# Two row tiles for the first MoE's turned rows, row stores ahead of the loads, and an earlier load of the branch value

## The chip, the cores and the metric

The kernel runs on one core of one Trainium2 chip. The metric is the device time of one execution in microseconds (us); three runs of the kernel before gave 932.9, 933.44 and 936.52, median 933.44. The execution that the profile shows took 933.06, and its span (first to last instruction) is 930.8; the 2.3 between them lies outside the instructions.

## The reference, cut to what matters

Attention over 4 batches of 12 heads (448 tokens, head size 64) with capped scores, then a dense gated MLP ("first MoE", 768 to 1536 to 768), then a routed MoE with 8 experts. All in float32.

```
scores = cap * tanh(q @ k.T / 8 / cap); attn = softmax(scores); x = attn @ v     # cap = 30
x = (silu(x @ w_gate) * (x @ w_val)) @ w_out                                    # 1792 x 768
do = x @ w_skip > 0; e = argmax(x[do] @ w_route); g = softmax prob of e
out = x;  out[do] += g * (relu(x[do] @ w1[e]) @ w2[e])
```

## The kernel before, in words

**Staging.** The 48 heads are worked in 24 pairs. The dense MLP works on one batch (448 tokens) at a time, in 36 units per batch: 12 of gate, 12 of value, 12 of output columns (6 blocks of 128 columns, each in two halves, in the order y00 y10 y01 y11 y20 y21 ...). A unit is 18 matmuls of 448 columns, since each product is made of three (high by high, low by high, high by low; `mm3`, L680 to L683). The attention of the next batch is woven between the units of this one, so that TensorE always has one or the other.

**The weights.** In the first batch they come as raw 64-bit words, 768 KB a unit (`load_w`, L629). ScalarE takes the absolute value (L639), VectorE clamps (L643) and puts the bits together (L648, L651, L654), and the 32-bit weight is kept in DRAM (`keep_w`, L678). Later batches load it from there, two units at a time (L620). Of each weight, ScalarE makes the rounded part wh (L668) and VectorE the rest wl (L356), both two units ahead of their product.

**The rows.** When an output block of 128 columns is done, ScalarE copies it out of PSUM (x2, L728). `turn_rows` (L747) lets TensorE make its routing logits (L751) and VectorE transpose it in 32 by 32 blocks into a tile "row" (L756). One unit later `store_rows` (L758) sends the row to the output with four transfers from SyncE's queue, 56 KB each, in runs of 32 floats (L762). Before the change the pool behind "row" has one buffer, so the transpose of the next block waits until the four stores of the block before have landed.

**What sets the order.** There is no scheduler: each engine works its instructions off in the order in which the program issues them. The order is written out by hand in lists of words. `OPENING` starts the first pairs; `unit(w)` (L1125) goes through `FIRST_UNITS` in the first batch and `UNITS` afterwards, and calls the function that stands behind each word in `place` (L1108). "store" is `store_rows` for the block that ended three units back, "rows" is `turn_rows` for the one that ended two back, "piece", "keep" and "loads" issue the loads of weights, the keeping of them and the loads of q, k and v. All of these transfers go out on SyncE's one queue, in program order, and each of them waits for the transfer eight before it. The sums of the softmax of a pair come from TensorE (L548), VectorE turns them (dn, L573) and TensorE spreads them again (L579); all further work of TensorE stands behind that matmul.

**The start.** The first pair's q and k are transposed by TensorE (L1287) and copied (L1290). Then each engine loads the value `big` (is the cap large?) into a register (L1291) and branches on it (L1292); with a cap of 30 the branch goes to `whole(False)`.

Of the kernel before, what the change touches and what calls it, by code (L numbers as in the profile page):

```python
# [7 lines left out]
F32 = mybir.dt.float32  # L8
# [41 lines left out]
""".split()  # L50
FIRST_UNITS = """
    out weigh sum scores1 roundw bits gate hidden after after after bits loww dn products both bits tanh1 exp1
    tanh2 exp2 turn abs bits split last bits scores2 bits piece keep loads logits count rows chain turnl store
""".split()
UNITS = """
    out turnl weigh sum scores1 scores2 products fold count logits rows hidden split loads tanh1 exp1 add1 turn
# [13 lines left out]
def tile_attn_moe_moe(  # L70
# [15 lines left out]
    nc = tc.nc  # L86
    B, H, S, D = q.shape
# [22 lines left out]
    big_i = const.tile([128, 1], I32, name="big_i")  # L110
# [15 lines left out]
    count = const.tile([T, E], F32, name="count")  # L126
# [9 lines left out]
    rows = const.tile([T, 128], mybir.dt.bfloat16, name="rows")  # L136
# [226 lines left out]
    def load_block(g, i):  # L363


        b, h = divmod(2 * g, H)
        a, j, e = i // 4, i // 2 % 2, i % 2
        qkn = block_of(g)
        p0 = 64 * j + 32 * e
        nc.sync.dma_start(  # L370
            out=qkn[p0:p0 + 32, a],
            in_=(q, k)[a][b, h + j, :, 32 * e:32 * e + 32].rearrange("(c i) d -> i c d", i=32),
        )
        return qkn

    def first_pair():
        return head_room[0:T, 0:2 * NC * 128].rearrange("p (a c h d) -> p a c h d", a=2, c=NC, h=2)

    def first_turned():
        return pair_room[1][:, 2 * S:4 * S].rearrange("p (a s) -> p a s", a=2)  # L380

    def whole(exact):
        with ExitStack() as ph:
# [13 lines left out]
            one_p = pool("one", 1)  # L397
# [287 lines left out]
            cur, terms = {}, {}  # L685
# [61 lines left out]
            def turn_rows(b, j):  # L747
                x2 = cur.pop(("x2", j))
                cur["lp", j] = lp = ps_m.tile([128, T], F32, name="mo")
                for c in range(NC):  # L750
                    nc.tensor.matmul(  # L751
                        lp[32 * c:32 * c + 32], lhsT=w9[:, j], rhs=x2[:, T * c:T * c + T], start=True, stop=True
                    )

                cur["row", j] = row = so["row"] if b == B - 1 and j % 2 else one_p.tile([128, S], F32, name="row")
                nc.vector.transpose(out=row, in_=x2)  # L756

            def store_rows(b, j):  # L758
# [58 lines left out]
            chain = [None, None]  # L817
# [13 lines left out]
            so = {"raw": [], "pair": [], "xg": [], "auto": False}  # L831
# [269 lines left out]
            def chain_on(w):  # L1101
# [10 lines left out]
                "scores1": of_head(1, scores, 3), "scores2": of_head(5, scores, 4),  # L1112
                "products": lambda w: w < W_END and products(w), "count": lambda w: step("p", 1),
                "logits": of_rows(add_logits, 3), "turnl": of_rows(turn_logits, 4), "rows": of_rows(turn_rows, 2),
                "store": of_rows(store_rows, 3), "split": split_due, "last": split_last, "loads": loads,
                "chain": chain_on, "tanh1": of_head(0, tanh, 2), "exp1": of_head(0, exp, 2),
# [24 lines left out]
            for word in OPENING:  # L1141
                name = word.rstrip("0123456789")
# [92 lines left out]
    with tc.manual_schedule():  # L1235
        nc.sync.dma_start(out=cap_sb, in_=cap.to_broadcast([128, 1]))
        for i, (queue, src) in enumerate(((nc.sync, q), (nc.scalar, k))):
            for j in range(2):
                queue.dma_start(out=first_pair()[:, i, :, j], in_=src[0, j].rearrange("(c p) d -> p c d", c=NC))
        for i in range(8):  # L1240
            load_block(1, i)
        nc.gpsimd.memset(ident, 1.0)
        nc.gpsimd.affine_select(
            out=ident, in_=ident, pattern=[[1, 128]], compare_op=ALU.is_equal, fill=0.0, base=0,
            channel_multiplier=-1,
        )
        nc.vector.memset(ones, 1.0)
        nc.scalar.activation(out=old, in_=ones[0:T, 0:1], func=ACTF.Tanh)
        nc.vector.tensor_reduce(
            alike[:, 0], ident.rearrange("p (a b) -> p b a", b=32), axis=AX.X, op=ALU.add  # L1250
        )
        nc.vector.tensor_copy(alike[:, 1], alike[:, 0])
        nc.vector.memset(w9, 0.0)
        nc.vector.tensor_scalar(big_i, cap_sb, cap_sb, CAP_FAST * CAP_FAST, op0=ALU.mult, op1=ALU.is_gt)
        nc.vector.tensor_scalar(inv_sb, cap_sb, float(D) ** 0.5, None, op0=ALU.mult)
        nc.vector.reciprocal(inv_sb, inv_sb)

        with tc.tile_pool(name="setup", bufs=5) as setup:

            def count_off(dst, **kw):  # L1260
                ti = setup.tile(list(dst.shape), I32, name="ti")
                nc.gpsimd.iota(ti[:], **kw)
                nc.vector.tensor_copy(dst, ti)

            count_off(rank8, pattern=[[-1, E]], base=E, channel_multiplier=0)
            count_off(rows, pattern=[[1, 128]], base=1, channel_multiplier=0)
            count_off(steps, pattern=[[128, JM]], base=0, channel_multiplier=0)
            count_off(slots, pattern=[[1, MAXSLOT]], base=0, channel_multiplier=0)
            nc.vector.tensor_scalar(number, rank8, -1.0, float(E), op0=ALU.mult, op1=ALU.add)
            nc.vector.tensor_tensor(  # L1270
                before, rank8.unsqueeze(1).to_broadcast([T, E, E]), rank8.unsqueeze(2).to_broadcast([T, E, E]),
                op=ALU.is_gt,
            )

            count_off(tok, pattern=[[T, NT]], base=-65536, channel_multiplier=1)
            nc.gpsimd.memset(oh, 0.0)
            nc.gpsimd.memset(above, 0.0)
            nc.gpsimd.affine_select(
                out=lt, in_=ones[0:T], pattern=[[1, T]], compare_op=ALU.is_ge, fill=0.0, base=0,
                channel_multiplier=-1,  # L1280
            )

        with tc.tile_pool(name="first", bufs=2, space=PSUM) as first_p:
            for i in range(2):
                ps = first_p.tile([128, S], F32, name="turned")
                for c in range(NC):
                    nc.tensor.transpose(  # L1287
                        ps[:, T * c:T * c + T], first_pair()[:, i, c].rearrange("p h d -> p (h d)"), ident[0:T, 0:T]
                    )
                (nc.scalar.copy if i else nc.vector.tensor_copy)(first_turned()[:, i], ps)  # L1290
        big = nc.values_load(big_i[0:1, 0:1], min_val=0, max_val=1)  # L1291
        with tc.If(big > 0) as cmp:  # L1292
            whole(True)
        with cmp.Else():
            whole(False)
# [31 lines left out]
```

## Time and profile before

| what | value |
|---|---|
| median of three runs | 933.44 us (932.9 to 936.52) |
| the profiled execution | 933.06 us, span 930.8 |
| TensorE busy | 897.0 us, 96% of the span |
| VectorE, ScalarE, GpSimd busy | 68%, 55%, 13% |
| mean granted TensorE clock | 0.985 |
| chain that ended last | 89% of it TensorE |

How to read it: TensorE is the engine that the time hangs on, so what counts is where it is not busy or its granted clock is under 1.00. Idle time of another engine costs something only where TensorE comes to wait for it. Times in rows are from the span's start.

### The profile page before, as it was taken

To read this page: it belongs to the slowest core of one execution; us is meant where nothing else is said; L and a number is where in the kernel's file an instruction comes from. 1 tells how busy PE (TensorE), PEld (TensorE's weight loads), DVE (VectorE), ACT (ScalarE), POOL (GpSimd) and SP (SyncE) were. 2 spreads that over 40 slices of the span, in tenths; PEclk is the share of its full clock that TensorE was granted. 3 is DMA by queue.
4 is the path that set the end of the run, shared out by engine and by line. 5 is a ranking of instruction groups with operands and counts; after the bars stand their busy time and mean duration, and the time that the engine had idled before them with its cause. 6 is when DMAs were issued, how large, how long until landed. Compare 5 with 4: busy or idle time off the path is not lost.

```text
span 930.8 us, 12697 instructions
## 1 busy us (share of the span) xinstructions
PE 897.0 (96%) x4708; PEld 700.5 (75%) x4708; DVE 635.2 (68%) x916; ACT 509.0 (55%) x587; POOL 124.3 (13%) x76
## 2 busy tenths in 40 slices
PE   5999999999899999999999999999999995999996
PEld 2336776677567877777777877889999885988996
DVE  1868999897736755736566664446755458899994
ACT  5996675666355455545554546233333432778883
POOL 1000000000002221122302223000000036311001
PEclk9999999999899999999999999999999997899999
DMA  6996888888668234432744222453364373999940
GB/s 125 212 239 180 232 247 245 234 230 242 155 128 199 79 93 128 98 93 62 180 120 127 88 93 68 97 129 137 118 226 165 81 217 126 378 392 397 395 178 7
DMA packets 226336, 161.50 MB, mean 174 GB/s; under 512 B 159180, under 2 KB 186828, under 8 KB 226256
## 3 DMA queue, kind: packets, MB, share of 16 engines
q1 hardware_dynamic: 224048, 157.12, 58.8%
q0 software_dynamic: 1280, 3.16, 0.9%
q8 instruction: 41, 0.67, 0.3%
q14 instruction: 39, 0.32, 0.1%
q10 hardware_dynamic: 928, 0.23, 0.1%
HBM read 140.80 MB, written 22.81 MB: 176 GB/s over the span
## 4 chain that ended last, share of the span: by engine, by line
PE 89%; DVE 3%; ACT 3%; SPq 2%; issue 1%; DMA 1%; POOL 0%; POOLq 0%; DVEq 0%
PE mo L681 20%; PE mo L682 19%; PE mo L683 19%; PE ps L459 7%; PE bank L514 6%; PE py L936 2%; PE py L934 2%; PE py L935 2%; PE ph L934 2%; PE ph L935 2%; PE ph L936 2%; PE mo L548 1%; SPq L370 1%; PE tp L885 1%; PE mo L751 1%
## 5 line engine op out<-in xcount | busy, mean ns | idle before, releaser
L681 PE MATMUL mo<-xhl,wh 128*128 128x448 f32 x576 | 215.0, 373 | 0.0
L683 PE MATMUL mo<-xhl,wl 128*128 128x448 f32 x576 | 210.4, 365 | 0.0
L682 PE MATMUL mo<-xhl,wh 128*128 128x448 f32 x576 | 210.3, 365 | 0.0
L356 DVE TENSOR_TENSOR wl<-raw,wh 128x768 fp32r<-128x768 f32 x108 | 115.3, 1068 | 76.4 <-ACT wh L668 75.0
L668 ACT CAST wh<-raw 128x768 fp32r<-128x768 f32 x108 | 89.7, 831 | 87.5 <-PE mo L682 62.6
L681 PEld LDWEIGHTS mo<-xhl,wh 128*128 128x128 f32 x576 | 108.1, 188 | 27.3 <-issue 8.1
L683 PEld LDWEIGHTS mo<-xhl,wl 128*128 128x128 f32 x576 | 108.2, 188 | 8.9 <-DVE wl L356 0.2
L682 PEld LDWEIGHTS mo<-xhl,wh 128*128 128x128 f32 x576 | 108.3, 188 | 7.9
L681 PE MATMUL mo<-hh,wh 128*128 128x448 f32 x288 | 108.4, 376 | 1.0 <-ACT x L728 1.0
L682 PE MATMUL mo<-hl,wh 128*128 128x448 f32 x288 | 105.5, 366 | 0.0
L683 PE MATMUL mo<-hh,wl 128*128 128x448 f32 x288 | 105.4, 366 | 0.0
L720 ACT ACTIVATE s<-mo 128x448 f32<-128x448 f32 x48 | 26.0, 541 | 114.3 <-PE mo L683 111.4
L459 PE MATMUL ps<-qkt 64*112 64x448 f32 x368 | 82.6, 568 | 0.0
L503 POOL TENSOR_TENSOR sums<-arena 112x896 f32<-112x896 f32 x11 | 23.2, 2113 | 393.4 <-ACT arena L475 393.4
L468 ACT ACTIVATE arena<-ps,inv_sb 112x896 f32<-112x896 f32 x72 | 68.7, 1006 | 5.4 <-PE ps L459 5.3
L475 ACT ACTIVATE arena<-arena,cap_sb 112x1792 f32<-112x1792 f32 x36 | 64.5, 1793 | 1.1
L681 PEld LDWEIGHTS mo<-hh,wh 128*128 128x128 f32 x288 | 54.3, 188 | 14.0 <-issue 7.9
L356 DVE TENSOR_TENSOR gl<-raw,gh 128x1536 fp32r<-128x1536 f32 x33 | 57.7, 1757 | 6.4 <-ACT gh L915 5.8
L723 DVE SCALAR_TENSOR_TENSOR s<-s,mo 128x448 f32<-128x448 f32 x48 | 29.6, 617 | 42.8 <-PE mo L683 42.5
L683 PEld LDWEIGHTS mo<-hh,wl 128*128 128x128 f32 x288 | 54.2, 188 | 4.6
L682 PEld LDWEIGHTS mo<-hl,wh 128*128 128x128 f32 x288 | 54.3, 188 | 4.0
L514 PE MATMUL bank<-arena,arena 112*64 112x448 f32 x264 | 54.9, 548 | 1.7 <-ACT arena L475 0.8
(241 smaller groups left out, 1434.3 us busy)
## 6 DMA issues: line engine op xcount, KB each, us to landing
raw<-ws SPq DMA_DIRECT2D x54, 768.0 KB, 4.6
raw<-in_moe_w_dram SPq DMA_DIRECT2D x33, 768.0 KB, 12.5
ws<-w SPq DMA_DIRECT2D x36, 384.0 KB, 5.8
more<-in_moe_w_dram SPq DMA_DIRECT2D x15, 768.0 KB, 13.2
raw<-in_moe_w_gate_dram SPq DMA_DIRECT2D x12, 768.0 KB, 5.6
raw<-in_moe_w_val_dram SPq DMA_DIRECT2D x12, 768.0 KB, 5.7
raw<-in_moe_w_out_dram SPq DMA_DIRECT2D x12, 768.0 KB, 5.3
pair_room<-in_moe_w_dram SPq DMA_DIRECT2D x11, 768.0 KB, 12.9
```

The source lines that it names most:

```text
L356: engine.tensor_tensor(low, full, high.bitcast(F32), op=ALU.subtract)
L459: nc.tensor.matmul(ps[:, i, 0:S], lhsT=qkt[rows_, 1, T * c:T * c + T], rhs=qkt[rows_, 0], start=True, stop=True)
L468: nc.scalar.activation(out=t[:, j], in_=ps[:, :, 0:S], func=ACTF.Tanh, scale=inv_sb[0:T])
L475: nc.scalar.activation(out=ts[part], in_=ts[part], func=ACTF.Exp, scale=cap_sb[0:T])
L514: nc.tensor.matmul(pv[64 * i:64 * i + 64], lhsT=hd["vn"][:, i, c], rhs=hd["t"][c // 2][:, c % 2, i], start=c == 0, stop=c == NC - 1,)
L668: nc.scalar.copy(wh, w32s[w])
L681: nc.tensor.matmul(ps, lhsT=wh, rhs=mh, start=start, stop=False)
L682: nc.tensor.matmul(ps, lhsT=wh, rhs=ml, start=False, stop=False)
L683: nc.tensor.matmul(ps, lhsT=wl, rhs=mh, start=False, stop=stop)
L934: nc.tensor.matmul(ps, lhsT=sh, rhs=wh, start=start, stop=False)
L935: nc.tensor.matmul(ps, lhsT=sh, rhs=wl, start=False, stop=False)
L936: nc.tensor.matmul(ps, lhsT=sl, rhs=wh, start=False, stop=stop)
```

## The change

Three edits. The row tile of the first MoE gets two buffers in place of one, in all batches (the rows of odd blocks of the last batch go to a tile of their own, as before). In `FIRST_UNITS`, the list of the first batch, the word "store" moves from the end to the place ahead of "piece", "keep" and "loads"; four of that batch's six blocks are stored under this list, the last two under `UNITS`, where nothing moves. The load of the value for the branch moves ahead of the turning of the first pair.

```
 FIRST_UNITS = """
     out weigh sum scores1 roundw bits gate hidden after after after bits loww dn products both bits tanh1 exp1
-    tanh2 exp2 turn abs bits split last bits scores2 bits piece keep loads logits count rows chain turnl store
+    tanh2 exp2 turn abs bits split last bits scores2 bits store piece keep loads logits count rows chain turnl
 """.split()
...
-                cur["row", j] = row = so["row"] if b == B - 1 and j % 2 else one_p.tile([128, S], F32, name="row")
+                cur["row", j] = row = so["row"] if b == B - 1 and j % 2 else one_p.tile([128, S], F32, name="row", bufs=2)
...
+        big = nc.values_load(big_i[0:1, 0:1], min_val=0, max_val=1)
 
         with tc.tile_pool(name="first", bufs=2, space=PSUM) as first_p:
...
-        big = nc.values_load(big_i[0:1, 0:1], min_val=0, max_val=1)
         with tc.If(big > 0) as cmp:
```

VectorE, at the second row of the first batch (row_11571 before, row_11575 now; x2_11486 is its block; the names in brackets are the semaphores that the instruction waits for, DMAHW those of the transfers):

```order
 L769 COPY lgt_66<-mo_11523 128x112 [waits PE_49]
-L756 STREAM_TRANSPOSE row_11571<-x2_11486 128x448 [waits DMAHW3_49,DMAHW4_49,DMAHW2_49,DMAHW1_49]
+L756 STREAM_TRANSPOSE row_11575<-x2_11486 128x448
 L643 TENSOR_SCALAR w32_11481<-w32_11481 128x768 [waits DMAHW7_49]
 L648 TENSOR_SCALAR w32_11481<-w32_11481 128x768 [waits DVE_49]
 L356 TENSOR_TENSOR wl_11583<-w32_11479,wh_11579 128x768 [waits PE_49,Activation_49]
```

No VectorE instruction changes its place; the transpose no longer waits for the four stores of the first row.

SyncE's queue at the same place (raw32 are weights for the second batch, ws the kept weights, pair_room takes q and k, arena3 v, row_11528 is the first block's row):

```order
-L620 DMA raw32_11558<-ws_60 128x2x768
+L762 DMA out_0_dram<-row_11528 32x14x32 x4
+L620 DMA raw32_11562<-ws_60 128x2x768
 L678 DMA ws_60<-w32_11479 128x768
 L370 DMA pair_room1_94<-in_k_dram 32x14x32 x4
-L762 DMA out_0_dram<-row_11528 32x14x32 x4
+L762 DMA out_0_dram<-row_11575 32x14x32 x4
 L678 DMA ws_60<-w32_11481 128x768
 L370 DMA pair_room0_93<-in_q_dram 32x14x32 x2
 L441 DMA arena3_9811<-in_v_dram 112x8x64
-L762 DMA out_0_dram<-row_11571 32x14x32 x4
```

The first row's stores move ahead of one load of 768 KB, one weight to be kept and four parts of k; the second row's move ahead of one kept weight, two parts of q and one v.

TensorE at the start (turned is the transposed first pair, big_i the value for the branch; VectorE, ScalarE and GpSimd load it at the corresponding place):

```order
 L1321 UNCONDITIONAL_BRANCH
-L1287 MATMUL turned<-ident,head_room 128x112 x8
-L1291 TENSOR_LOAD big_i
+L1282 TENSOR_LOAD big_i
+L1288 MATMUL turned<-ident,head_room 128x112 x8
 L1292 COMPARE_AND_BRANCH
```

The load of the value changes places with the eight transposes; on SyncE it stays where it was, behind the eight loads of the second pair.

## Rows read from the trace of the kernel before

**Rows 1.** Waits, 215 to 275 us: engine, line, releaser: total, times, longest.

```profile
DVE row L756 <- DMA out_dram<-row: 10.4, 2, 9.6
```

**Rows 2.** Windows: length, busy (x instructions) by engine, granted clock, DMA share, GB/s.

```profile
241.00:251.00 10.00, 5.82 (x26) 2.97 (x26) 9.30 (x16) 6.04 (x7) 0.00 (x0) 0.66 0.73 160
251.00:760.00 509.00, 509.00 (x2663) 414.12 (x2665) 293.27 (x469) 231.86 (x292) 80.88 (x39) 1.00 0.46 123
760.00:800.00 40.00, 29.99 (x132) 26.86 (x133) 34.35 (x60) 15.39 (x16) 24.52 (x15) 0.79 0.58 202
```

**Rows 3.** Timeline of VectorE: start, duration of one, line, what [idle before <-releaser].

```profile
228.34 0.27 DVE L769 COPY lgt<-mo 128x112 f32<-128x112 f32 x1
238.22 0.65 DVE L756 STREAM_TRANSPOSE row<-x 128x448 f32<-128x448 f32 x1 [9.62 <-DMA out_dram<-row]
...
244.66 0.64 DVE L573 STREAM_TRANSPOSE dn<-mo 128x448 f32<-128x448 f32 x1
```

**Rows 4.** Timeline of SyncE, transfers issued: start, time over all of them.

```profile
225.15 1.46 SPq L370 DMA_DIRECT2D pair_room<-in_q_dram  x2
228.49 0.39 SPq L620 DMA_DIRECT2D raw<-ws  x1
...
232.23 4.38 SPq L762 DMA_DIRECT2D out_dram<-row  x4
```

**Rows 5.** Timeline of TensorE, 226 to 251 us.

```profile
226.87 0.47 PE L681 MATMUL mo<-hh,wh 128*128 128x448 f32 x1 [0.97 <-ACT x L728]
...
227.58 0.36 PE L681 MATMUL mo<-hh,wh 128*128 128x448 f32 x1
...
236.34 0.94 PE L548 MATMUL mo<-head_room,ones 112*32 112x448 f32 x8
...
240.81 0.37 PE L683 MATMUL mo<-hh,wl 128*128 128x448 f32 x1
245.36 0.40 PE L579 MATMUL bank<-dn,alike 64*64 64x14 f32 x4 [4.18 <-DVE dn L573]
...
249.48 0.74 PE L681 MATMUL mo<-hh,wh 128*128 128x448 f32 x1
...
250.72 0.37 PE L681 MATMUL mo<-hh,wh 128*128 128x448 f32 x1
```

**Rows 6.** Chain of waits, 225 to 300 us: start, length, what.

```profile
245.76 0.53 PE mo L751 x8
246.29 3.26 PE ps L459 x8
...
276.31 0.22 PE bank L579 x4
276.53 1.69 PE ps L459 x8
...
282.07 0.33 PE mo L751 x8
```

**Rows 7.** Timeline of ScalarE, two instructions that wait for loads.

```profile
229.45 0.89 ACT L639 ACTIVATE w<-raw 128x768 f32<-128x768 f32 x1 [0.16 <-DMA raw<-in_moe_w_out_dram]
...
258.59 0.83 ACT L668 CAST wh<-raw 128x768 fp32r<-128x768 f32 x1
```

**Rows 8.** DMA issues of the page: count, KB each, median us to landing.

```profile
raw<-ws SPq DMA_DIRECT2D x54, 768.0 KB, 4.6
```

**Rows 9.** Instructions of line 1291: duration ns, start.

```profile
L1291 PEldq TENSOR_LOAD <-big_i x1: 497/497/497, 6.4 to 6.4; - x1
L1291 SPq TENSOR_LOAD <-big_i x1: 470/470/470, 7.0 to 7.0; - x1
```

**Rows 10.** Timeline of all engines, 0 to 34 us.

```profile
11.00 5.44 PE L459 MATMUL ps<-pair_room 64*112 64x448 f32 x16 [3.06 <-issue]
...
20.16 1.38 SPq L629 DMA_DIRECT2D raw<-in_moe_w_val_dram  x1
...
26.05 0.94 ACT L639 ACTIVATE w<-raw 128x768 f32<-128x768 f32 x1 [0.85 <-DMA raw<-in_moe_w_val_dram]
```

More of the change, by code (lines that the diff above doesn't have):

```diff
@@ L52 @@
     out weigh sum scores1 roundw bits gate hidden after after after bits loww dn products both bits tanh1 exp1
-    tanh2 exp2 turn abs bits split last bits scores2 bits piece keep loads logits count rows chain turnl store
+    tanh2 exp2 turn abs bits split last bits scores2 bits store piece keep loads logits count rows chain turnl
 """.split()
@@ L753, in turn_rows @@
                     )
-                cur["row", j] = row = so["row"] if b == B - 1 and j % 2 else one_p.tile([128, S], F32, name="row")
+                cur["row", j] = row = so["row"] if b == B - 1 and j % 2 else one_p.tile([128, S], F32, name="row", bufs=2)
                 nc.vector.transpose(out=row, in_=x2)
@@ L1281, in tile_attn_moe_moe @@
             )
+        big = nc.values_load(big_i[0:1, 0:1], min_val=0, max_val=1)
         with tc.tile_pool(name="first", bufs=2, space=PSUM) as first_p:
@@ L1290, in tile_attn_moe_moe @@
                 (nc.scalar.copy if i else nc.vector.tensor_copy)(first_turned()[:, i], ps)
-        big = nc.values_load(big_i[0:1, 0:1], min_val=0, max_val=1)
         with tc.If(big > 0) as cmp:
```

## The prediction

> **What bounds the kernel now.** I read the busy shares first (TensorE 96%, the chain that ended last 89% TensorE), so only places count where TensorE idles or its clock falls. The waits come next, since the change takes one away: VectorE's row transpose waits 10.4 us for row stores, in two waits, one of them 9.6 [rows 1]. The windows say what that stretch costs and whether the time would be kept afterwards: from 241 to 251 us TensorE is busy 5.82 of 10 at a mean clock of 0.66, while from 251 to 760 it is busy 509.00 of 509 at 1.00 [rows 2]. So what is won before 251 has nothing behind it that could swallow it before 760. The timelines then give cause and order. VectorE is through at 228.34 + 0.27 = 228.61 and starts the transpose of the second row at 238.22 [rows 3]. The first row's stores, which it waits for, were issued only from 232.23, since SyncE issued a load at 228.49, a kept weight and four parts of k ahead of them [rows 4]. TensorE had work until 240.81 + 0.21 = 241.02 (a matmul of 448 columns follows the one before it by some 0.2 there) and went on at 245.36, after a wait of 4.18 for VectorE's dn transpose [rows 5].
>
> **Part one: two buffers and earlier stores.** No work is added or removed: 24 row transposes and 96 stores before and after. What goes is the wait of 9.62 [rows 3].
>
> *Term 1, the idle time.* TensorE's wait before L579 is 4.18 [rows 5].
>
> *Term 2, the slow clock behind it.* The same instructions took longer after the idle time than at a clock of 1.00. L579 x4: 245.36 to 245.76, 0.40 against 0.22. Logits L751 x8: 0.53 against 0.33. Scores L459 x8: 3.26 against 1.69 [rows 5, 6]. First three matmuls of the next product: 249.48 to 250.72, 1.24, against 226.87 to 227.58, 0.71 [rows 5]. The differences are 0.18, 0.20, 1.57 and 0.53, sum 2.48. TensorE ran just before with no gap, at full clock, so with the idle time the fall should go too.
>
> Sum: 4.18 + 2.48 = 6.66.
>
> *What is late next.* VectorE needed 245.30 - 238.22 = 7.08 from the start of that transpose to the end of dn [rows 3]. Started at 228.61 it could be there at 235.7, but dn reads the sums that TensorE ends at about 236.34 + 0.94 = 237.28 [rows 5]. So dn ends near 237.9, and TensorE asks for it at 241.02: 3.1 to spare. VectorE will now wait for TensorE and no longer the other way round. The wl that the next product wants stands between the transpose and dn on VectorE, so it is there before 235.7, against a need at 241.02 + 0.22 + 0.33 + 1.69 = 243.3.
>
> *What the moved stores push back.* They are issued when the two parts of q are out, 225.15 + 1.46 = 226.6 [rows 4]; their row was ready at 224.6. SyncE issued nothing from there to 228.49 anyway. Four stores took 4.38 to issue here [rows 4], so the load behind them goes out by about 231, which is 2.5 later. It is first read at 258.59 in the kernel before, without a wait [rows 7]; that is 251.9 when all is 6.66 earlier. Such loads land 4.6 us after their issue in the median [rows 8]; with twice that, 9.2, some 11 us are left. So this costs nothing, and the cover is large. The raw load that ScalarE waited 0.16 for at 229.45 [rows 7] was issued before the stores. If they slow it by their whole 4.38, the absolute value is done at 229.45 + 4.38 + 0.89 = 234.7, the wh behind it (0.83) at 235.6, wl about 1 us later, and dn still by 238. The kept weight behind the second row's stores no longer waits for VectorE's late start.
>
> A rule that speaks against the move is in the Trainium skill, "DMA: Bandwidth & Descriptors", section "Queues, rings and completion order": on each engine descriptors are consumed in ring order, so a big load behind many small pieces starts behind them; its section "Specifications" puts the size for full rate at 512 B, and a row store has runs of 128 B. No row here shows a load behind such stores. By the rule the load's landing, and not only its issue, moves back; the sum by it would be the same 6.66 as long as the 11 us of cover hold, but whoever goes by it would give rival 1 some 0.1 in place of the 0.07 below.
>
> The row tile takes 448 more floats a partition and moves the tiles behind it; the order of SyncE's instructions shows no wait added in the late stage. I take 0 for that.
>
> **Part two: the earlier value.** TensorE's load of the value took 0.497 at 6.4, between transposes and branch [rows 9]; the first scores came at 11.00, 3.06 after the last transpose [rows 10]. Ahead of the transposes the load falls into the time in which TensorE waits for q, so branch and scores can come 0.5 sooner. Nothing of it should last: at 26.05 ScalarE waits 0.85 for a weight load that SyncE issued at 20.16 [rows 10], and SyncE's own load of the value, at 7.0 [rows 9], stands where it stood. Whatever ScalarE has won by then it loses at that load. Bounds: -0.5 (all of it kept) and +0.5 (the same again lost, if five engines that fetch the code behind the branch at other times get in each other's way). I take 0, the row at 26.05 being the nearest.
>
> **Sum.** 933.06 - 6.66 = 926.4 for the profiled execution. That one was 0.38 under the median of 933.44; on the median it is 926.8. I predict 926.6.
>
> **The rivals.**
>
> *1. Part of the wait stays.* The stores slow the raw load that landed at 229.4, ScalarE stands in front of it, and the wh, wl and dn behind it come late. From that landing to the end of dn it is some 3.5 us (0.89 and 0.83 of [rows 7], about 1 for wl, 0.64 for dn), so TensorE idles before 241.02 only if the load is late by more than about 8. If half the idle time and all the slow clock stay: 926.4 + 2.1 + 2.5 = 931.0. For it: stores, loads and kept weights now meet in the same few us. Against: the load was issued first.
>
> *2. The late stage gives it back.* Between 760 and 800 TensorE is busy 29.99 of 40 at a mean clock of 0.79 [rows 2]; with the levels 1 and 0.5 that is 0.42 x 40 = 16.8 us at the low one, which cost up to 8.4. Shifted by 6.66, the same pauses may meet other falls and rises of the clock. If a third of the 8.4 comes on top or goes: 926.4 + 2.8 = 929.2, or 923.6. For it: of the stretches of rows 2 behind 251 it is the one whose clock is not 1.00. Against: its work and its pauses are unchanged.
>
> *3. The start pays*: 926.6 - 0.5 = 926.1.
>
> *4. Slower: the wait moves to SyncE.* Stores ahead of loads mean that SyncE stands in front of a store until VectorE has transposed the row, with the weight loads behind. Place: the load at 228.49. It decides only when that load is later than its 11 us of cover; from there each us costs one, and 2.5 more for the clock. If each of the four moved groups of stores held the queue for as long as VectorE once stood (9.62), the loads behind would be 38.5 late: 926.4 + 27.5 + 2.5 = 956. Against: the row is ready 2 us before SyncE gets there.
>
> *5. No change*: the wait was for something else that also came at 238: 933.4. Against: no wait stands at that transpose any more, and its other input was there.
>
> **Chances.** The forecast 0.77 (with its own range 925.2 to 928), rival 1 0.07, rival 2 0.06, rival 3 0.06, rival 4 0.02, rival 5 0.02. About 0.5% (4.7 us) is what a measurement of this kernel can tell from no change, so faster means under 928.8. Forecast and rival 3 are faster, half of rival 2 as well, and a little of rival 1: 0.87. Same: most of rivals 1 and 2, and 5: 0.10. Slower 0.03. The range is 924.8 to 929.3: downwards rival 3 and a part of what the late stage's clock may win, upwards the milder half of rivals 1 and 2.
>
> **What would show it.** Right: no wait of a row transpose for stores near 228 and the transpose at about 228.6; stores of the first row issued near 226.7; TensorE without a gap from 227 to 260 at clock 1.00, L579 at 241.0; VectorE's dn waiting for L548; first scores at about 10.5, but the absolute value that stood at 26.05 still waiting for its load, longer than before. Wrong: a wait of ScalarE for raw weights of more than 4 us near 230, a low clock between 240 and 251, or a difference that first shows behind 760.

## The result and the profile after

| | before | after |
|---|---|---|
| device time, median (range), us | 932.62 (931.27 to 936.52, 6 runs) | 924.89 (923.51 to 927.18, 6 runs) |
| profiled execution: time, span, us | 933.06, 930.8 | 927.18, 924.8 |
| mean granted clock of TensorE | 0.985 | 0.990 |

The ratio is 0.9915, with a 95% interval of 0.9895 to 0.9935: 7.7 us faster, where the forecast of 926.6 stood 6.8 under the median of 933.44. The six runs of the kernel before are the three of that median and three more (931.88, 931.27, 932.33). The changed kernel was measured twice more beside the kernel before, at 0.9913 [0.9901, 0.9926] and 0.9916 [0.9901, 0.9932]; the three differences are 7.7, 7.5 and 7.9 us. 924.89 lies at the lower edge of the range (924.8 to 929.3) and below the forecast's own range (925.2 to 928).

The windows of the kernel after, with the columns of [rows 2] and one stretch more in front:

```profile
225.00:241.00 16.00, 14.52 (x86) 8.79 (x85) 13.48 (x22) 10.39 (x12) 0.00 (x0) 1.00 0.85 221
241.00:251.00 10.00, 10.00 (x59) 7.88 (x58) 9.68 (x16) 3.76 (x6) 0.00 (x0) 1.00 0.94 232
251.00:760.00 509.00, 508.43 (x2665) 413.22 (x2664) 291.25 (x474) 231.15 (x291) 83.18 (x42) 1.00 0.46 122
760.00:800.00 40.00, 28.98 (x133) 25.79 (x133) 35.28 (x52) 18.38 (x20) 23.88 (x12) 0.83 0.63 233
```

From 241 to 251 us TensorE is busy 10.00 of 10 at a clock of 1.00, where [rows 2] had 5.82 at 0.66. Behind 251 the two kernels are alike until 760, but for 0.57 us of idle time. The stretch from 225 to 241 holds 1.48 us of idle time that the timeline names. Rows from the timelines of its engines, put in order of time (they answer to [rows 3, 4, 5, 7]; start, duration of one, engine, line, what, and in brackets the idle time before it and who ended it):

```profile
226.96 0.40 PE L751 MATMUL mo<-x,w 128*32 128x112 f32 x8
...
227.14 1.42 SPq L370 DMA_DIRECT2D pair_room<-in_q_dram  x2
...
227.46 0.90 ACT L639 ACTIVATE w<-raw 128x768 f32<-128x768 f32 x1
...
228.26 0.52 ACT L728 COPY x<-mo 128x448 f32<-128x448 f32 x1
...
228.66 3.64 SPq L762 DMA_DIRECT2D out_dram<-row  x4
...
228.84 0.47 PE L681 MATMUL mo<-hh,wh 128*128 128x448 f32 x1 [1.48 <-ACT x L728]
...
230.33 0.27 DVE L769 COPY lgt<-mo 128x112 f32<-128x112 f32 x1
...
230.51 0.64 DVE L756 STREAM_TRANSPOSE row<-x 128x448 f32<-128x448 f32 x1
...
231.48 0.93 ACT L639 ACTIVATE w<-raw 128x768 f32<-128x768 f32 x1 [0.20 <-DMA raw<-in_moe_w_out_dram]
...
232.41 0.43 SPq L620 DMA_DIRECT2D raw<-ws  x1
...
239.31 0.65 DVE L573 STREAM_TRANSPOSE dn<-mo 128x448 f32<-128x448 f32 x1 [2.28 <-PE mo L548]
...
243.08 0.29 PE L579 MATMUL bank<-dn,alike 64*64 64x14 f32 x4
...
252.82 0.40 PE L751 MATMUL mo<-x,w 128*32 128x112 f32 x8
...
253.85 0.83 ACT L668 CAST wh<-raw 128x768 fp32r<-128x768 f32 x1
```

The second row's transpose (230.51) follows the copy ahead of it with no wait. VectorE now waits for TensorE (2.28 before dn), dn is ready at 239.31 + 0.65 = 239.96, and TensorE asks for it at 243.08, 3.1 later, without a wait. The four stores were issued ahead of the load L620, which went out at 232.41 and was read at 253.85 without a wait. What is left is TensorE's 1.48 before L681, for ScalarE's copy x.

The opening, same columns (answers to [rows 10]):

```profile
10.22 3.33 PE L459 MATMUL ps<-pair_room 64*112 64x448 f32 x8 [2.28 <-issue]
...
21.50 0.56 SPq L629 DMA_DIRECT2D raw<-in_moe_w_val_dram  x1
...
27.59 0.92 ACT L639 ACTIVATE w<-raw 128x768 f32<-128x768 f32 x1 [1.95 <-DMA raw<-in_moe_w_val_dram]
```

The first scores start 0.78 sooner, and ScalarE then waits 1.95 for w_val where it waited 0.85. The longer wait is not the time won: ScalarE comes to this load at 25.64, not earlier than before (25.20), and the load was issued 1.34 later.

### The profile page after: what moved, and what is told of

Its sections match the earlier page's. It is cut to its first block, busy times and chain, and to the rows that moved or that the text cites. A ratio compares the mean times of both kernels' runs of the same rounds, so it can differ in the third digit from the quotient of the medians.

```text
span 924.8 us, 12699 instructions
## 1 busy us (share of the span) xinstructions
PE 892.4 (96%) x4708; PEld 697.0 (75%) x4708; DVE 635.0 (69%) x916; ACT 509.2 (55%) x587; POOL 124.1 (13%) x76
## 4 chain that ended last, share of the span: by engine, by line
PE 90%; DVE 3%; ACT 3%; SPq 2%; issue 1%; DMA 1%; POOL 0%; POOLq 0%; ACTq 0%
PE mo L681 20%; PE mo L683 19%; PE mo L682 19%; PE ps L459 7%; PE bank L514 7%; PE py L936 2%; PE py L934 2%; PE py L935 2%; PE ph L934 2%; PE ph L935 2%; PE ph L936 2%; PE mo L548 2%; SPq L370 1%; PE tp L885 1%; PE mo L751 1%
## 5 line engine op out<-in xcount | busy, mean ns | idle before, releaser
L681 PE MATMUL mo<-xhl,wh 128*128 128x448 f32 x576 | 215.0, 373 | 0.0
L668 ACT CAST wh<-raw 128x768 fp32r<-128x768 f32 x108 | 89.8, 831 | 87.4 <-PE mo L682 62.5
L681 PEld LDWEIGHTS mo<-xhl,wh 128*128 128x128 f32 x576 | 108.1, 188 | 27.3 <-issue 8.9
L681 PE MATMUL mo<-hh,wh 128*128 128x448 f32 x288 | 108.1, 375 | 1.5 <-ACT x L728 1.5
L681 PEld LDWEIGHTS mo<-hh,wh 128*128 128x128 f32 x288 | 54.0, 188 | 13.8 <-issue 6.6
```

The source lines that it names most:

```text
L668: nc.scalar.copy(wh, w32s[w])
L681: nc.tensor.matmul(ps, lhsT=wh, rhs=mh, start=start, stop=False)
```

## One stretch that adds up

All experiments are read by one stretch of TensorE: from its logits of row 1 (L751 at 226.96 above) to those of row 3 (252.82). In the kernel before these stand at:

```profile
225.50 0.40 PE L751 MATMUL mo<-x,w 128*32 128x112 f32 x8
...
257.62 0.40 PE L751 MATMUL mo<-x,w 128*32 128x112 f32 x8
```

That is 32.12 us, against 25.86 after. Three things happen in it: the wait of L681 for ScalarE's copy x (never under 0.29), the wait of L579 for VectorE's dn, and the lower clock. All profiled executions, in us (in the two dose kernels lines are one higher; the place of row 1's logits and the last two columns add up to that execution's span):

| kernel | row 1's logits at | wait for x | wait for dn | clock fell to half | row 1 to row 3 | row 3 to span end |
|---|---|---|---|---|---|---|
| before | 225.50 | 0.97 | 4.18 | behind dn | 32.12 | 673.2 |
| value only (e3) | 225.71 | 0.29 | 4.89 | behind dn | 32.08 | 673.2 |
| after | 226.96 | 1.48 | 0 | no | 25.86 | 672.0 |
| after (e5) | 225.83 | 1.00 | 0 | no | 25.38 | 673.1 |
| after (e12) | 226.79 | 0.93 | 0 | no | 25.31 | 671.8 |
| buffers only (e1) | 228.70 | 0.29 | 0 | no | 24.67 | 673.1 |
| stores only (e2) | 226.33 | 0.30 | 0 | no | 24.67 | 671.7 |
| stores only (e11) | 227.76 | 1.86 | 0 | behind x | 27.81 | 673.0 |
| both row edits (e4) | 226.76 | 2.42 | 0 | behind x | 28.38 | 672.4 |
| both row edits (e6) | 225.29 | 1.90 | 0 | behind x | 27.77 | 673.0 |
| dose of 4 (e8) | 228.24 | 0.29 | 1.65 | no | 26.39 | 673.3 |
| dose of 6 (e10) | 227.38 | 0.29 | 2.23 | no | 26.97 | 673.5 |
| Abs late (e7) | 228.02 | 0.74 | 0 | no | 25.13 | 671.8 |
| w_val early (e9) | 228.58 | 1.18 | 0 | no | 25.54 | 673.0 |

Where the clock stays up, row 1 to row 3 is 24.67 + (wait for x - 0.29) + (wait for dn), within 0.07 in all nine. Where it falls behind the wait for x, 1.5 to 1.6 come on top, for example in e11: 27.81 - 24.67 - 1.57 = 1.57.

## The experiments

### The change taken apart (e1 to e4)

e1, two buffers alone:

```diff
-... one_p.tile([128, S], F32, name="row")
+... one_p.tile([128, S], F32, name="row", bufs=2)
```

> Two row buffers alone; stores where they were, behind the loads; value loaded where it was. Theory A (the only cost was VectorE standing before the second row, TensorE asks for dn 3.1 us after it can be ready): the whole stage gain of 6.7 us, ratio 0.9928; VectorE starts the second row's transpose right behind the copy of the logits, TensorE has no gap at L579. Theory B (each edit of the rows gives a part, the stores behind the loads still hold something up): about half, 3 to 4 us, ratio 0.996. Theory C (the earlier value gives the 1 us by which the change beat the 6.7): here 1 us less than with all three edits, at 925.9 where that has 924.9.

Measured: 926.08 us, ratio 0.9922 [0.9904, 0.9940]; no wait at the second transpose.

e2, the place of the stores alone:

```diff
-    tanh2 exp2 turn abs bits split last bits scores2 bits piece keep loads logits count rows chain turnl store
+    tanh2 exp2 turn abs bits split last bits scores2 bits store piece keep loads logits count rows chain turnl
```

> Stores ahead of the loads alone; one row buffer, so the second row's transpose still waits for the first row's four stores. Theory A: the stores go out from 226.6 and land by about 233, so VectorE resumes near 233 in place of 238.2; it needs 7.08 to the end of dn, 240.1, and TensorE asks at 241.0. So the wait of VectorE stays at about 4.5 us and costs nothing: again 6.7 us, ratio 0.9928. If the stores land after 234 each us costs one; after 236 or so the slow clock comes back with 2.5. Theory B: about half, 0.996. Theory D (stores slow when they share the queue with the big load): no gain, ratio 1.000.

Measured: 925.21 us, ratio 0.9921 [0.9902, 0.9940]. Timeline of e2:

```profile
226.92 3.90 SPq L762 DMA_DIRECT2D out_dram<-row  x4
...
233.55 0.65 DVE L756 STREAM_TRANSPOSE row<-x 128x448 f32<-128x448 f32 x1 [4.58 <-DMA out_dram<-row]
...
239.99 0.64 DVE L573 STREAM_TRANSPOSE dn<-mo 128x448 f32<-128x448 f32 x1
...
241.26 0.29 PE L579 MATMUL bank<-dn,alike 64*64 64x14 f32 x4
```

e3, the value load alone:

```diff
+        big = nc.values_load(big_i[0:1, 0:1], min_val=0, max_val=1)
         with tc.tile_pool(name="first", bufs=2, space=PSUM) as first_p:
...
-        big = nc.values_load(big_i[0:1, 0:1], min_val=0, max_val=1)
```

> The earlier load of the branch value alone. Theory A: first scores 0.5 to 0.8 us earlier (10.2 to 10.5 in place of 11.0), but the absolute value at 26 waits for its load all the same: 0 us, ratio 1.000 within 0.001. Theory C: 0.5 to 1 us faster, ratio 0.999 or less. Theory E (the opening of the changed kernel was 1.5 us late at that load in its profile, 27.6 in place of 26.05, and the change is the reason): 1.5 us slower, ratio 1.0016, with that absolute value again at 27 or later.

Measured: 932.99 us, ratio 0.9990 [0.9976, 1.0004]. Timeline of e3:

```profile
25.43 0.93 ACT L639 ACTIVATE w<-raw 128x768 f32<-128x768 f32 x1 [0.60 <-DMA raw<-in_moe_w_val_dram]
...
238.48 0.65 DVE L756 STREAM_TRANSPOSE row<-x 128x448 f32<-128x448 f32 x1 [10.13 <-DMA out_dram<-row]
...
245.62 0.40 PE L579 MATMUL bank<-dn,alike 64*64 64x14 f32 x4 [4.89 <-DVE dn L573]
```

e4, both row edits without the value load (the diffs of e1 and e2 together):

> Both edits of the rows without the earlier value: the change less its third part. Theory A: 6.7 us, ratio 0.9928, the opening as before with the absolute value at 26. Theory C: 1 us slower than all three edits. Theory E: 1.5 us faster than all three edits, and the opening back at 26.05. Theory B: the same as all three edits, and the two single ones well behind it.

Measured: 928.09 us, ratio 0.9946 [0.9927, 0.9965].

What follows: each row edit by itself gives all of the gain, so A holds there and halves (B) fall. D falls, since e2 gained, and E, since e3 was not slower and its Abs stood at 25.43. C (the earlier value brings 1 us) is not decided: 926.08 in e1 and 0.9990 in e3 fit it, but A allowed 0.9990 too, and e4 lies 3.2 us above the kernel after, not 1. With one buffer and early stores VectorE still waits 4.58, and this costs nothing, since dn ends 241.26 - 240.63 = 0.63 before TensorE uses it. The value load alone is anything from 0.4 us slower to 2.2 faster by its interval, 0.9 faster at its middle. e4 was slower than its parts, and its timeline shows by what:

```profile
213.66 1.50 SPq L629 DMA_DIRECT2D raw<-in_moe_w_out_dram  x1
...
221.87 0.92 ACT L639 ACTIVATE w<-raw 128x768 f32<-128x768 f32 x1 [4.91 <-DMA raw<-in_moe_w_out_dram]
...
228.21 0.90 ACT L639 ACTIVATE w<-raw 128x768 f32<-128x768 f32 x1
...
229.01 0.51 ACT L728 COPY x<-mo 128x448 f32<-128x448 f32 x1
...
229.57 0.48 PE L681 MATMUL mo<-hh,wh 128*128 128x448 f32 x1 [2.42 <-ACT x L728]
```

and its windows:

```profile
228.00:230.00 2.00, 0.43 (x2) 0.41 (x3) 2.00 (x3) 1.52 (x3) 0.00 (x0) 0.99 0.82 217
230.00:233.00 3.00, 3.00 (x10) 2.68 (x9) 2.93 (x7) 1.53 (x2) 0.00 (x0) 0.50 1.03 296
```

The raw w_out issued at 213.66 came at 221.8; ScalarE waited 4.91 for it (3.25 in e2, whose load was issued at 212.34 and landed by 218.96), ran without a pause from there, and made the copy x late. TensorE waited 2.42, and the clock was at half for three us. None of this lies behind an edit of e4. A's 0.9928 stands at the edge of its interval.

### The same kernels again (e5, e6)

e5 is the kernel after and e6 is e4's kernel, unchanged.

> The kernel after, unchanged, to see how far two builds of the same text lie apart on another chip and how its opening scatters. Theory S (scatter: the profiled opening and the wait for ScalarE's copy x differ from run to run by 1 to 3 us whatever the edit): a median of 924 to 926.5 us, a ratio of 0.990 to 0.994, TensorE's product L681 behind the logits of row 1 waits 0.3 to 2.4 us for ACT x L728, and L579 waits nothing. Theory V (the earlier value is worth 3 us once the row edits are in): 924 to 925.5 here and 927.5 to 929 for the same kernel without it.

> Both row edits without the move of the value load, a second time, beside the kernel after on one chip. Theory S: within 1 us of the kernel after in this call (924 to 926.5 us); the 928.1 of the first time came from its opening and from a wait of 2.4 us for ACT x L728 that brought the lower clock, and the wait measures 0.3 to 1.5 this time. Theory V: 2 to 4 us above the kernel after again (927 to 929), with the wait of 2.4 us and the lower clock behind it back in the same place.

Measured: e5 925.75 us (0.9913 [0.9901, 0.9926]), e6 926.79 us (0.9934 [0.9918, 0.9951]). They lie 1.04 apart: nearer to theory S than to V's 2 to 4, but e6 is over the 926.5 that S allowed, and its wait for x was 1.90, not 0.3 to 1.5, with the lower clock behind it, as V had it. Left open here.

### ScalarE's Abs behind the copy (e7)

```diff
-    out weigh sum scores1 roundw bits gate ...
-    tanh2 exp2 turn abs bits split ...
+    out weigh sum scores1 roundw abs bits gate ...
+    tanh2 exp2 turn bits split ...
```

> The kernel after, with ScalarE's Abs of the raw weights (L639) in the first units issued behind the rounding of the unit (roundw) and no longer ahead of the copy of x2 (L728). Theory G: the copy no longer stands behind a wait of 3 to 5 us for raw w_out, so TensorE's L681 behind the logits waits 0.3 us at most where the kernel after has 1.48; from the logits of row 1 to those of row 3 it takes 24.7 us (25.9 in the kernel after): 0.5 to 1.2 us less than the kernel after again, 923.7 to 924.5 us. Rival H: VectorE gets each w 1 to 1.5 us later and frees the raw buffers later, the loads that refill them start later, and ScalarE or TensorE waits for w or wh instead: the same time as the kernel after or 1 to 4 us more, 925 to 929 us.

Measured: 927.33 us, ratio 0.9936 [0.9922, 0.9949]. Timeline of e7:

```profile
227.77 0.92 ACT L639 ACTIVATE w<-raw 128x768 f32<-128x768 f32 x1
...
228.59 0.52 ACT L728 COPY x<-mo 128x448 f32<-128x448 f32 x1
...
229.16 0.47 PE L681 MATMUL mo<-hh,wh 128*128 128x448 f32 x1 [0.74 <-ACT x L728]
```

G falls: an Abs (the one now issued behind the rounding ahead) still stands in front of the copy, the wait shrank only to 0.74, and the whole is 1.6 us slower than e5. That is in H's range, and H's wait is there: ScalarE's rounding L668 waits 0.48 us at 221.32 and 0.44 at 227.03 for VectorE's w, where the kernel after has no wait at 222.38 and 226.74. The stretch itself is no longer than in e5 (25.13 against 25.38), so in the profiles the loss lies ahead of it (row 1's logits at 228.02 against 225.83).

### Doses on VectorE's wait (e8, e10)

The stores-only kernel, with more stores of row 0 into a spare tensor, so that the second transpose waits for them too:

```diff
+    spare = dram.tile([S, 128], F32, name="spare")
...
+                if b == 0 and j == 0:
+                    for i in range(4):
+                        nc.sync.dma_start(
+                            out=spare[:, 32 * i:32 * i + 32].rearrange("(a p) d -> p a d", p=32),
+                            in_=row[32 * i:32 * i + 32].rearrange("p (a d) -> p a d", d=32),
+                        )
```

> The store move alone (one row buffer), with four more stores of row 0 into a spare tensor in DRAM behind the real four: VectorE's second row transpose waits for them too. A dose between the store move alone (a wait of 4.58 us, which cost nothing: dn ended 0.6 us before TensorE used it) and the kernel before (9.62 us). Theory D (each us past the cover is one us of TensorE, and the idle time then brings the lower clock): four issues of 0.9 to 1.0 us more make that wait 8.2 to 8.5 us, L579 waits 2.9 to 3.3 us for dn, and with 0 to 2.5 us of lower clock the time is 928.3 to 931 us, 3 to 5.8 us above the store move alone (925.2 in the first call). Rival Q (the stores run side by side, so that their landing and not their issue counts): the wait grows by under 1.5 us, L579 waits 0 to 1 us, 925 to 926.5 us. The raw load and the loads of k that stand behind the stores on SyncE start 3.6 us later, and by both theories cost nothing.

e10 is the same with six stores and a spare tensor 192 wide:

> The store move alone, with six more stores of row 0 into a spare tensor in DRAM (four of them made a wait of 6.90 us on VectorE, 1.65 us on TensorE at L579, a full clock behind it, and 929.36 us). By what four stores measured (3.31 us), two more make 1.7 us: VectorE waits 8.4 to 8.8 us, L579 waits 3.2 to 3.5 us. Theory D with the clock (an idle time of that length brings the lower clock, as 4.18 us did in the kernel before): the granted clock falls to half behind L579 and the time is 932 to 934 us, 2.6 to 4.6 us above the four stores. Rival D1 (only the idle time counts, the clock stays): 930.8 to 931.4 us, with a granted clock of 1.00 behind L579.

Measured: e8 929.36 us (928.75 to 929.96), ratio 0.9956 [0.9944, 0.9969]; e10 929.82 us (928.07 to 933.23, 12 runs), ratio 0.9968 [0.9953, 0.9983]. Timeline of e8:

```profile
232.80 3.31 SPq L769 DMA_DIRECT2D spare<-row  x4
...
237.76 0.65 DVE L757 STREAM_TRANSPOSE row<-x 128x448 f32<-128x448 f32 x1 [6.90 <-DMA spare<-row]
...
244.89 0.29 PE L580 MATMUL bank<-dn,alike 64*64 64x14 f32 x4 [1.65 <-DVE dn L574]
```

and its window:

```profile
241.00:251.00 10.00, 8.35 (x50) 6.28 (x49) 9.30 (x16) 6.04 (x7) 0.00 (x0) 1.00 0.96 232
```

Timeline and windows of e10:

```profile
231.87 3.77 SPq L770 DMA_DIRECT2D spare<-row  x6
...
237.48 0.65 DVE L757 STREAM_TRANSPOSE row<-x 128x448 f32<-128x448 f32 x1 [7.47 <-DMA spare<-row]
...
244.62 0.29 PE L580 MATMUL bank<-dn,alike 64*64 64x14 f32 x4 [2.23 <-DVE dn L574]
```

```profile
241.00:251.00 10.00, 7.77 (x47) 5.78 (x46) 9.32 (x16) 6.04 (x7) 0.00 (x0) 1.00 0.96 239
```

VectorE's wait less TensorE's is 5.25 in e8, 5.24 in e10, and 10.13 - 4.89 = 5.24 in e3: the first 5.24 us of VectorE's wait are free, and each us past them is a us of TensorE. (The kernel before has 9.62 - 4.18 = 5.44, with a wait for x of 0.97 in place of 0.29.) That is D's mechanism, with smaller doses than forecast (6.90 where 8.2 to 8.5 stood, 7.47 where 8.4 to 8.8 stood). Q falls. At 1.65 and 2.23 us of idle time the clock stayed at 1.00; the dose of 3.2 to 3.5 us that was to show where it falls was not reached, so e10 doesn't tell its two theories apart. The times rose by more (4.2 us from e2 to e8) than the 1.72 that the stretch shows; of the rest, later starts (228.24 against 226.33) and 1.6 us behind row 3 stand in the table, and neither has a cause that the edit would explain. The two medians also come from different chips; by the ratios the step is 3.3.

### w_val ahead of the second pair (e9)

```diff
-    scores0 tanh0 values0 piece0 turn1 scores1 exp0 load2 tanh1 weigh0 scores2 abs0 exp1
-    values1 piece1 tanh2 ...
+    scores0 tanh0 values0 piece0 turn1 scores1 exp0 piece1 load2 tanh1 weigh0 scores2 abs0 exp1
+    values1 tanh2 ...
```

> The kernel after, with the first load of raw w_val issued by SyncE ahead of the second pair's eight loads of q and k (at about 12 us; 21.50 us in the kernel after). Theory O (the end of ScalarE's wait for that load, at 25.4 to 28.7 us in the runs so far, sets where the first MoE begins, and scatters the whole time): the second L639 of the opening starts without a wait at 25 to 26 us, TensorE's product L681 behind the logits of row 1 starts at 225.5 to 227.0 us (226.4 to 229.6 us in the ten profiled runs so far), and the time is 923 to 925.5 us, 0 to 2.5 us below the kernel after. Rival P (the pair's loads are what the opening lacks): the loads of q and k land later by the 768 KB in front of them, VectorE's transposes L449 of the second pair wait 2 to 5 us longer, and the time is 926 to 930 us.

Measured: 927.21 us (924.83 to 928.92), ratio 0.9932 [0.9913, 0.9951]. Timeline of e9:

```profile
24.50 0.90 ACT L639 ACTIVATE w<-raw 128x768 f32<-128x768 f32 x1
...
24.59 1.11 DVE L449 STREAM_TRANSPOSE qkt<-pair_room 128x896 f32<-128x896 f32 x1 [4.68 <-DMA pair_room<-in_k_dram]
...
230.15 0.47 PE L681 MATMUL mo<-hh,wh 128*128 128x448 f32 x1 [1.18 <-ACT x L728]
```

and of the kernel after:

```profile
22.89 1.11 DVE L449 STREAM_TRANSPOSE qkt<-pair_room 128x896 f32<-128x896 f32 x1 [1.95 <-DMA pair_room<-in_k_dram]
```

ScalarE's wait for w_val is gone, but VectorE waits 4.68 for k (1.95 in the kernel after), and the first MoE's place is reached at 230.15, later than in any other profiled run. O's forecast falls, P's holds. That the opening is short of what its loads bring in all, and not of this one, fits this but is argued. O's premise stands in the rows all the same: in the twelve profiles other than e7 and e9, row 1's logits come 199.4 to 200.3 us behind the start of the opening's second Abs, which waits for w_val (199.4 to 199.5 in ten of them), and that start scatters from 25.43 to 28.75. So the column "row 1's logits at" goes with the landing of that load.

### One edit against both, once more (e11, e12)

> The store move alone, a second time, beside the kernel after on one chip. In the profiled runs so far TensorE's product L681 behind the logits of row 1 waited 0.29 to 0.30 us for ScalarE's copy x (L728) in the four kernels with one row edit or a dose on it, and 0.74 to 2.42 us in the six that have both row edits, though nothing ahead of that place differs. Theory U (having both edits makes the copy late): 0.3 us again here, from the logits of row 1 to those of row 3 24.7 us, and a time 0.7 to 1.5 us below the kernel after. Theory S (scatter of the opening): the wait measures 0.3 to 2.4 us here, and the two kernels lie within 0.7 us, both at 924.5 to 926.5 us.

> The kernel after, a third time. Theory U: the wait of L681 for the copy x is 1.0 to 2.4 us again, and the time 925 to 927 us, 0.7 to 1.5 us above the store move alone. Theory S: the wait measures 0.3 to 2.4 us, and the time lies within 0.7 us of the store move alone. By both, from the logits of row 1 to those of row 3 it takes 24.67 us, plus the wait above 0.29, plus what the lower clock adds where it falls (0 to 1.6 us).

Measured: e11 926.20 us (0.9917 [0.9902, 0.9932]), e12 925.50 us (0.9916 [0.9901, 0.9932]). Timeline and windows of e11:

```profile
217.03 0.92 ACT L639 ACTIVATE w<-raw 128x768 f32<-128x768 f32 x1 [0.72 <-DMA raw<-in_moe_w_out_dram]
...
222.32 0.92 ACT L639 ACTIVATE w<-raw 128x768 f32<-128x768 f32 x1 [4.37 <-DMA raw<-in_moe_w_out_dram]
...
230.02 0.47 PE L681 MATMUL mo<-hh,wh 128*128 128x448 f32 x1 [1.86 <-ACT x L728]
```

```profile
231.00:234.00 3.00, 3.00 (x10) 2.68 (x9) 0.79 (x2) 1.74 (x2) 0.00 (x0) 0.52 1.10 293
```

U falls: the kernel that had waited 0.30 for x waits 1.86 here, with the clock at half behind it. S holds: 1.86 and 0.93, with medians 0.70 apart. The wait for x differs between two executions of one kernel, and the rows show what it goes with: ScalarE's waits for raw w_out (L639) 7 to 13 us ahead of that copy. They sum to 3.2 or 3.3 us in the five profiles in which L681 waited 0.29 or 0.30 (e1, e2, e3, e8, e10), to 4.2 to 4.7 where it waited 0.93 to 1.48 (before, after, e5, e9, e12), and to 4.9 to 5.1 where it waited 1.86 to 2.42 (e4, e6, e11: 0.72 + 4.37). These loads are issued ahead of the first row's stores, so no store was moved in front of them. What makes them land late stays open. Whether having both row edits makes it likelier (all seven such profiles waited over 0.7, against one of five with one edit) is not settled either. No version beat the kernel after; the stores-only kernel (925.21, 926.20) and the buffers-only kernel (926.08) are as fast within what these runs tell.

## What the prediction had right, and the step that failed

*The bound and the cause.* Right. The wait of 9.62 went, with it TensorE's 4.18 and the lower clock behind, and between 251 and 760 us no more than 0.57 of it was given back.

*Term 1, 4.18.* This is the step that failed, by its size. It took the wait as a fixed 4.18, read from one execution, and the 0.97 us that TensorE had waited for x [rows 5] as untouched, a cost that stays in the kernel before and after. But in the kernel before that wait was free: VectorE set the end of the stretch, and it takes 32.12 with waits of 0.97 for x and 4.18 for dn, and 32.08 with 0.29 and 4.89 (e3). With VectorE out of the way TensorE sets it, and each us of the wait for x counts. So the term is 4.9 when the copy x is on time, and the edit then wins 32.1 - 24.67 = 7.4 in the stretch (e1, e2), not 6.66. It wins less by what the wait for x measures above 0.29: 6.3 to 6.8 in the three profiled executions of the kernel after, where 6.66 is thus met within 0.4, and 3.7 to 4.3 in e4, e6 and e11, where the wait brought the lower clock.

*The late stage at 0.* The sum had nothing for it, and in the profile of the kernel after it gave 1.2 us (row 3 to span end, 673.2 to 672.0). It goes with the granted clock from 760 to 800 us: the mean is 0.83 to 0.87 in the four profiles with 671.7 to 672.0 (after, e2, e7, e12), and 0.79 in the ten others (672.4 to 673.5), the kernel before among them. Why an execution gets the one or the other is open.

*What of the miss is not settled.* The profiled pair differs by 933.06 - 927.18 = 5.9 where 6.66 were forecast: row 1 came 1.46 later, the stretch won 6.26 and the late stage 1.2. That the forecast came out near this pair is in part luck, since the first and the last were not in its sum. The median, 924.89, lies 1.7 under the forecast. Of this, 0.8 is the base, 933.44 with three runs and 932.62 with six. The other 0.9 is gain (7.7 where 6.8 was forecast); the first interval, 6.1 to 9.8 us, holds 6.8 as well, that of e12 (6.3 to 9.2) too, that of e5 (6.9 to 9.2) just not. Of the twelve profiled executions with a row edit, ten lay above their kernel's median, on the average of the twelve by 1.2 us, while the kernel before's 933.06 lay within 0.5 of its first two medians (933.44 and 932.62). The least of each column among them, 225.29 + 24.67 + 671.7 = 921.7, is the span of the shortest run of the kernel after (921.7), so no place beyond the three columns is needed. But which column was short in the executions without a trace is not recorded, so how the 0.9 divides between term 1, the late stage and the start stays open.

*Term 2, 2.48.* Held. In e3 the stretch gives it again: 32.08 - 24.67 - 4.89 = 2.52.

*What is late next.* Held to the tenth: 3.1 us of spare for dn were forecast, and 243.08 - 239.96 = 3.1 measured. But "TensorE without a gap from 227 to 260" failed: a gap of 1.48 stands at the very wait that term 1 had passed over.

*The stores ahead of the load.* Held. L620 went out at 232.41, against row 1's logits 2.5 us later than before, as forecast, and was read at 253.85 with no wait; ScalarE's wait for raw w_out near 230 was 0.20 [0.16 in rows 7]. On each DMA engine descriptors are consumed in ring order, the Trainium skill states ("DMA: Bandwidth & Descriptors", section "Queues, rings and completion order"). A later landing by it, as the prediction worked it out, does not show here: behind four stores L620 landed 4.6 (e5), 4.8 (e12) and 6.0 us (e2) after its issue, behind eight 5.8 (e8), behind ten 5.6 (e10), and with the stores still behind it 5.0 (e1), 5.1 (before) and 5.7 (e3).

*Part two at 0.* The value load alone measured 0.9990 [0.9976, 1.0004]. The half us at the start is there: the first scores begin at 10.22 to 10.70 in the six profiles with the earlier load and at 10.78 to 11.21 in the eight without. That it is lost at the load of w_val, as the prediction had it, is not shown. In e3 the scores start 0.31 sooner and ScalarE's wait for w_val is shorter, 0.60 against 0.85; in the profile of the kernel after ScalarE had lost what it won before it came to that load, in a wait of 1.24 for w_gate at 19.45. The Abs behind w_val starts at 25.4 to 27.6 with the earlier value and at 25.9 to 28.8 without (e9 left out), a scatter that hides half a us. Beside the row edits it may bring something: the kernel after lies 1.0 (e5 to e6, one chip) to 3.2 us (first to e4, measured apart) below the same kernel without it, and 0.4 on average below e1, e2 and e11. No row shows where, so it stays open.

*The rivals.* 1: no part of the wait stayed. 2: it works, at about half the size given and as a gain: in the four profiles with the higher late clock it is 1.2 to 1.5 us less behind row 3 than in the kernel before, in the eight others with a row edit from 0.8 less to 0.3 more. 3 is neither shown nor excluded by e3's interval. 4: SyncE's stores held no load back past its cover, which eight stores did not use up. 5 fell with the first run.

## What to carry to other kernels

When two engines wait for each other in turns, take the gain of removing one wait from the whole stretch, marker to marker, and ask what the waits of the engine that is set free were worth under the old bound: those that were free before will count afterwards. A wait has a cover, a first part that costs nothing, here 5.24 us on VectorE; two ways of getting below it (another buffer, or earlier stores) are worth the same and don't add up. Profile the same text more than once before a difference of a per cent or less is put down to an edit.

## What was not expected of the hardware

- The length of an idle time alone did not decide whether the clock fell. Behind 1.86, 1.90 and 2.42 us of waiting for x the granted clock went to half (0.50 in e4 from 230 to 233); behind 1.65 and 2.23 us of waiting for dn it stayed at 1.00 from 241 to 251 (e8, e10). What differed before the two places was not tried.
- Issuing stores of this shape on SyncE had no fixed price: four took 4.38 us in the kernel before [rows 4], 3.64 after, 3.31 for the spare ones in e8, and six took 3.77 in e10 (0.63 each). A dose counted in stores therefore missed its size twice.
